# Another hand-written order of the same 2034 steps, with other engines for some splits and other buffers

## The chip, the cores and the metric

One NeuronCore of a Trainium2 chip runs the whole program. The metric is the device time of one execution in microseconds (us). Several executions are made; their median is the figure, and one further execution is recorded by the hardware profiler.

## The reference, cut to what matters

Two stages follow each other. In the first, for each of 8 batches and 8 heads, 512 tokens `x` of width 64 read 32 state rows by a softmax, and the 32 state rows read the tokens back. The two results, side by side, are 544 rows of width 512 for a batch. In the second stage four experts with a causal attention of width 64 work on these rows; a gate picks the two best experts for each row.

```python
scores = scale * x @ state.T;  xread = softmax(scores) @ state
sread = softmax(scale * state @ x.T) @ x
X = concat([xread, sread])                       # 8 x 544 x 512
logits = X @ w_gate; pick 2 of 4 experts, w = softmax of the two
for e in range(4):
    q, k, v = X @ wq[e], X @ wk[e], X @ wv[e]
    ye = softmax(causal(scale * q @ k.T)) @ v @ wo[e]
    out += w[:, e] * ye                          # only where e was picked
```

## The kernel before

The program is a list of 2034 steps, written batch by batch by ordinary Python functions: `first` and `front` (stage one of a batch and its q, k, v), `probs` (scores and exponentials of a block of 128 rows), `reads` (their product with v), `outs` (the product with wo and the store), `side` (the state rows) and `tail` (attention of the state rows of two batches). Each step has a number, an engine, one or a few instructions, and the buffers that it reads and writes. For some steps there are two or three ways to do it, on different engines: a number in float16 is kept as a high half (a rounded copy) and a low half (what is left of it), and `split`, `low`, `small` and `copy` let either ScalarE, VectorE or GpSimd make such parts.

What is issued when is not decided by these functions. `Steps.run` (lines 346 to 362) goes through the string `ORDER` and issues the steps in the order of its numbers. An entry `1929.0` is step 1929 by its way 0; `388.0.5` puts five matmuls of zeros ahead of step 388, which keep TensorE busy. All engines take their own instructions from this one list in its order, and each engine works through its part strictly in turn. The string table `SLOTS` says which of a tag's buffers each use takes: `"z": "1010..."` gives the first use buffer 1, the next one buffer 0, and so on. Semaphores are set by the tile framework from what reads and writes what.

```python
for entry in order:
    s = self.all[int(entry[0])]
    calls = s["ways"][int(entry[1])][2]
```

SyncE (SP) issues all DMAs, 172 of them, from one queue: loads of x, state and weights, stores of the output, and the transposing DMAs that bring high and low halves into the layout that TensorE needs (`xT<-xh`, `a2t<-a2`, `qm<-qh`, `pt<-ph`, `z<-zh`, `tpt<-ptl`). TensorE's products of the scores wait for `qm`, those with v for `pt`, those with wo for `z`.

Steps that the prediction names, with what they do: 62 and 63 load `wq` (three experts, then one), 64 and 65 `wk`, 66 and 67 `wv`, 68 the gate's weights. 86, 83 and 89 multiply `wk`, `wq` and `wv` with the state of batch 0; 119 is the first matmul after stage one's softmax of batch 0. 753 is a product with v in batch 2. 1440 to 1442 and 1455 to 1458 make the exponentials of two row blocks of batch 5, their high and low halves and the transposing DMA; 1479 is the product that reads the second of them. In the last batch 1926 to 1929 are high half, low half, transposing DMA and the product with wo of row block 3; 1969 and 1972 are the halves of the product with wo of row block 0; 1753 and 1756 are the products with wo of two blocks of batch 6. 2020 to 2022 are high half, low half and transposing DMA of the last tail's exponentials (`ptl`, `tpt`), 2023 is the product that reads them, 2031 the last product with wo, 2032 its copy and 2033 its store.

Of the kernel before, what the change touches and what calls it, by code (L numbers as in the profile page):

```python
# [125 lines left out]
    "p32": "02110221110211020210210210210210211021002",  # L126
    "mb": "00010101",
    "sbm": "10010010",
    "m2": "00001101",
    "bd": "0101010",  # L130
    "kt": "021012012",
    "gs1": "1001001010101",
# [1059 lines left out]
```

## Time and profile before

| | us |
|---|---|
| median of 3 executions | 288.12 (287.46 to 291.04) |
| profiled execution, its own time | 290.49 |
| its span, first to last instruction | 288.7 |
| granted TensorE clock, mean share of full speed | 0.994 |

The span is what the trace covers; 1.8 us of the execution's own time lie around it. A busy share of an engine is a mean over the whole span. The page of the profile gives busy times, a picture of the span in 40 slices, and the chain of waits that ended last. The other views ask the same trace for single stretches, engines and buffers.

### The profile page before, as it was taken

To read this page: it belongs to the slowest core of one execution; us is meant where nothing else is said; L and a number is where in the kernel's file an instruction comes from. 1 tells how busy PE (TensorE), PEld (TensorE's weight loads), DVE (VectorE), ACT (ScalarE), POOL (GpSimd) and SP (SyncE) were. 2 spreads that over 40 slices of the span, in tenths; PEclk is the share of its full clock that TensorE was granted. 3 is DMA by queue.
4 is the path that set the end of the run, shared out by engine and by line. 5 is a ranking of instruction groups with operands and counts; after the bars stand their busy time and mean duration, and the time that the engine had idled before them with its cause. 6 is when DMAs were issued, how large, how long until landed. Compare 5 with 4: busy or idle time off the path is not lost.

```text
span 288.7 us, 9583 instructions
## 1 busy us (share of the span) xinstructions
PE 270.6 (94%) x3571; PEld 182.2 (63%) x3573; DVE 242.5 (84%) x778; ACT 215.5 (75%) x707; POOL 197.9 (69%) x271
## 2 busy tenths in 40 slices
PE   8799998899899996999999999999999999999984
PEld 4757745486458643779457666776756667576742
DVE  2679999999899999899989899989899768887620
ACT  4488899798888889588889879657988475357632
POOL 7526986789768896489969969967687436616100
PEclk9979999999999999999999999999999999999999
DMA  7959779999999999989999999998559939899474
GB/s 194 180 166 128 171 198 159 246 165 185 259 173 206 199 184 165 246 222 201 227 179 233 155 254 244 204 226 165 142 129 130 220 85 146 165 181 156 123 210 148
DMA packets 154575, 53.20 MB, mean 184 GB/s; under 512 B 140576, under 2 KB 150048, under 8 KB 154528
## 3 DMA queue, kind: packets, MB, share of 16 engines
q1 hardware_dynamic: 154528, 52.59, 95.9%
q8 instruction: 28, 0.46, 0.6%
q14 instruction: 19, 0.16, 0.2%
HBM read 11.02 MB, written 8.91 MB: 69 GB/s over the span
## 4 chain that ended last, share of the span: by engine, by line
PE 60%; DVE 13%; DMA 12%; POOL 4%; ACT 4%; issue 3%; SPq 3%; DVEq 0%; ACTq 0%; POOLq 0%
PE bank L362 60%; DMA pt<-ph 6%; SPq L362 3%; DMA p<-in_moe_wk_dram 2%; DVE bank L362 2%; DMA qm<-qh 2%; DVE m L362 1%; DMA tpt<-ptl 1%; DVE z L362 1%; DVE qf L362 1%; DVE eb L362 1%; POOL z L362 1%; DVE xh L362 1%; DVE gs L362 1%; ACT p L362 1%
## 5 line engine op out<-in xcount | busy, mean ns | idle before, releaser
L362 PE MATMUL bank<-kt,qm 128*128 128x128 f16 (+13 forms) x368 | 48.2, 313 | 1.9 <-DMA qm<-qh 1.3
L362 PE MATMUL bank<-gs,at 128*128 128x260 f16 (+3 forms) x368 | 49.6, 282 | 0.4 <-ACT kt L362 0.2
L362 PE MATMUL bank<-v,pt 128*128 128x192 f16 x480 | 44.3, 246 | 5.3 <-DMA pt<-ph 4.3
L362 PE MATMUL bank<-wo_n,z 128*128 128x512 f16 (+1 forms) x198 | 46.2, 373 | 0.7 <-DVE gs L362 0.4
L362 PEld LDWEIGHTS <-pt 128*128 128x128 f16 x480 | 40.1, 97 | 9.2 <-DMA pt<-ph 6.5
L362 POOL TENSOR_TENSOR ph<-p,ph 128x256 f16<-128x256 f32 (+3 forms) x27 | 37.9, 1407 | 5.5 <-ACT bank L362 2.5
L362 PEld LDWEIGHTS <-at 128*128 128x128 f16 x336 | 32.4, 98 | 7.5 <-issue 1.1
L362 DVE CUSTOM_DVE_ANT_0 bank<-bank,causal 128x256 f32<-128x256 f32 (+3 forms) x64 | 30.2, 506 | 6.2 <-PE bank L362 5.4
L362 ACT ACTIVATE p<-bank,mx 128x384 f32<-128x384 f32 (+3 forms) x64 | 33.3, 524 | 1.3 <-DVE mx L362 0.2
L362 PEld LDWEIGHTS <-qm 128*128 128x128 f16 (+1 forms) x336 | 20.2, 96 | 17.9 <-issue 5.9
L362 PEld LDWEIGHTS <-z 128*128 128x128 f16 x198 | 18.6, 98 | 18.9 <-issue 1.4
L362 ACT ACTIVATE o<-bank 128x512 f32<-128x512 f32 (+1 forms) x35 | 20.2, 582 | 9.0 <-PE bank L362 7.3
L362 PE MATMUL bank<-at,gs 128*128 128x512 f16 (+1 forms) x100 | 24.4, 381 | 0.1
L362 DVE SCALAR_TENSOR_TENSOR xh<-xn,xh 128x512 f16<-128x512 f32 x23 | 18.5, 815 | 5.0 <-ACT xh L362 4.9
L362 POOL TENSOR_TENSOR z<-z 128x128 f32<-128x128 f32 x24 | 12.1, 504 | 14.9 <-DVE z L362 13.7
L362 DVE TENSOR_TENSOR z<-bank,c 128x384 f32<-128x384 f32 x32 | 17.5, 548 | 5.3 <-PE bank L362 3.1
L362 ACT ACTIVATE xh<-xn 128x512 f16<-128x512 f32 x32 | 19.5, 629 | 2.8 <-DMA xn<-in_x_dram 2.8
L362 POOL TENSOR_SCALAR ph<-p 128x768 f16<-128x768 f32 (+3 forms) x13 | 10.5, 804 | 15.2 <-ACT p L362 8.6
L362 POOL TENSOR_TENSOR qh<-qf,qh 128x384 f16<-128x384 f32 x18 | 17.3, 970 | 4.9 <-ACT qh L362 3.9
L362 POOL TENSOR_TENSOR zh<-z,zh 128x256 f16<-128x256 f32 x22 | 15.6, 714 | 6.8 <-DVE zh L362 3.3
L362 POOL TENSOR_TENSOR a<-e,a 128x512 f16<-128x512 f32 x14 | 16.5, 1184 | 4.1 <-ACT a L362 3.8
L362 DVE SCALAR_TENSOR_TENSOR qf<-bank,m 128x384 f32<-128x384 f32 x32 | 17.3, 549 | 2.1 <-PE bank L362 1.3
(206 smaller groups left out, 645.4 us busy)
## 6 DMA issues: line engine op xcount, KB each, us to landing
out_dram<-o SPq DMA_DIRECT2D x33, 256.0 KB, 3.1
xn<-in_x_dram SPq DMA_DIRECT2D x14, 512.0 KB, 4.5
xn<-in_x_dram SPq DMA_DIRECT2D x4, 256.0 KB, 4.0
sn<-in_state_dram SPq DMA_DIRECT2D x8, 64.0 KB, 3.7
p<-in_moe_wo_dram SPq DMA_DIRECT2D x2, 256.0 KB, 3.6
xT<-xh SPq DMA_TRANSPOSE x28, 4.1
pt<-ph SPq DMA_TRANSPOSE x25, 4.6
p<-in_moe_wk_dram SPq DMA_DIRECT2D x1, 384.0 KB, 5.5
```

The lines of the kernel that those rows point to most:

```text
L362: f(**{k: v.ap() if isinstance(v, View) else v for k, v in kw.items()})
```

## The change

Only the strings `ORDER` and `SLOTS` differ. Both orders hold the same 2034 steps once each. 117 of them go another way than before: 32 from VectorE to GpSimd and 11 back, 14 from ScalarE to GpSimd and 17 back, 26 from ScalarE to VectorE and 17 back. The fillers of zeros ahead of step 119 (three) are gone, and those ahead of step 388 are two and not five. On TensorE 232 of the 306 steps keep their order among each other, on SP 115 of 172. The diff, cut to the first lines, the last lines and some of the slots:

```diff
 ORDER = """
-2.0 3.0 184.0 186.0 32.0 52.0 0.0 47.0 51.0 7.0 34.0 61.0 33.0 39.0 38.0 40.0 13.0 48.0 71.0 1.0 8.0 69.0 4.0 5.0 131.0 9.0 187.0 72.1 185.0 10.0
-188.0 70.0 189.0 133.0 132.1 190.0 191.0 64.0 198.0 134.0 62.0 66.0 65.0 204.0 201.0 73.0 74.0 75.0 45.0 76.0 135.0 86.0 136.0 77.0 63.0 67.0 68.0
-207.0 83.0 218.0 6.0 88.0 87.0 78.1 137.0 195.0 138.0 89.0 210.0 79.0 91.0 80.1 44.0 50.0 324.0 139.0 222.0 140.0 141.0 142.1 323.0 322.0 90.0 325.0
...
-2013.0 1746.1 1911.0 1912.1 2014.0 1739.0 2015.0 2016.0 2017.0 2018.0 2019.0 2020.0 1740.0 1981.0 1942.1 1737.0 1909.0 1923.0 1922.0 1939.1 1940.0
-1924.0 1752.0 1945.0 1277.0 1941.0 1741.0 1954.0 1925.1 1926.2 1927.0 1753.0 1946.0 1947.1 1948.0 1756.0 1963.0 1943.0 1944.1 2021.1 1955.0 1956.0
-1949.0 1982.0 1950.0 1957.0 1951.0 1754.0 1958.0 1964.0 1965.0 1928.0 1966.0 1929.0 1967.0 1757.0 1968.0 2022.0 1755.0 1546.0 1959.0 1930.0 2023.0
-1952.0 1758.0 1738.0 1960.0 2024.0 2025.0 2026.0 2027.0 2028.0 2029.0 2030.0 1961.0 1969.0 1970.0 1953.0 1931.0 1962.0 1971.0 1972.0 1973.0 1974.0
-2031.0 2032.0 2033.0
+0.0 3.0 45.0 13.0 2.0 7.0 184.0 71.0 72.0 186.0 4.0 5.0 69.0 1.0 133.0 8.0 131.0 185.0 70.0 188.0 9.0 10.0 190.0 187.0 134.1 73.0 66.0 67.0 64.0 65.0
+62.0 132.0 135.0 204.0 207.0 198.0 189.0 191.0 74.0 75.0 63.0 6.0 68.0 136.0 323.0 322.0 86.0 201.0 76.0 83.0 20.0 32.0 48.0 14.0 33.0 15.0 77.0 11.0
+218.0 195.0 87.0 137.0 89.0 78.1 79.0 80.1 84.0 88.0 138.0 85.0 210.0 90.0 139.0 140.1 222.0 324.0 81.0 82.0 119.0 333.0 327.0 336.0 141.0 91.1 142.1
...
+1736.0 1934.0 1743.0 1977.0 2011.1 2012.0 1917.1 1919.0 1935.0 1544.0 1982.0 1749.1 1918.0 1920.0 1936.1 1937.0 1744.0 1745.1 2013.0 1938.0 1939.0
+1921.1 1750.0 1912.0 1746.0 1909.0 1923.0 1945.0 1940.1 2015.0 2014.0 1737.0 1922.0 1739.0 1954.0 1751.0 1752.0 2016.0 2017.1 1924.0 1925.0 1926.2
+1946.0 1942.1 1947.1 1941.0 1927.0 1948.0 1753.0 2018.0 2019.0 2020.0 1963.0 1545.0 1943.0 2021.1 1944.1 1955.0 1956.0 1964.0 1965.1 1949.0 1950.0
+1756.0 1957.0 1966.0 1951.0 1738.0 2022.0 1757.0 1754.0 1740.0 2023.0 1958.0 1952.0 1967.0 1968.0 1928.0 2024.1 1959.0 2025.0 2026.0 2027.0 1546.0
+1929.0 1972.0 1758.0 1741.0 1930.0 2028.0 2029.0 1973.0 1953.0 1755.0 2030.0 1960.0 2031.0 1961.0 1974.0 1931.0 1962.0 2032.0 2033.0 1969.0 1970.0
+1971.0
 """
 SLOTS = {
...
-    "a2t": "01010100",
-    "zh": "101110010110101",
-    "z": "101010010110100100",
+    "a2t": "10100110",
+    "zh": "010110111000101",
+    "z": "011101011001101100",
...
```

Of the steps that the prediction names, in words: the weights are loaded in the order 64, 62, 66, 65, 63, 67, 68 before and 66, 67, 64, 65, 62, 63, 68 after. TensorE's last steps before are 1756, 1963, 1957, 1951, 1966, 1929, 2023, 1960, 2028, 1969, 1972, 2031; after they are 1963, 1756, 1957, 1966, 1951, 2023, 1929, 1972, 2028, 1960, 2031, 1969. SP's end has 1741, 1928, 2022 before and 1738, 2022, 1928 after. On GpSimd 1456 now follows 1442 and stands ahead of 1457; before, ScalarE did it.

## Rows read from the trace of the kernel before

**Rows 1.** The page: busy us (share) xinstructions; TensorE's clock in 40 slices.
```profile
PE 270.6 (94%) x3571; PEld 182.2 (63%) x3573; DVE 242.5 (84%) x778; ACT 215.5 (75%) x707; POOL 197.9 (69%) x271
PEclk9979999999999999999999999999999999999999
```

**Rows 2.** Waits of PE: line <- releaser: us in total, times, longest.
```profile
PE bank L362 <- DMA pt<-ph: 4.3, 3, 2.9
PE bank L362 <- DMA p<-in_moe_wk_dram: 1.9, 1, 1.9
PE bank L362 <- DMA qm<-qh: 1.3, 1, 1.3
PE bank L362 <- DVE gs L362: 1.3, 2, 0.9
PE bank L362 <- DVE rd L362: 1.1, 2, 0.6
```

**Rows 3.** Windows: PE, PEld, DVE, ACT, POOL busy, clock, DMA, GB/s.
```profile
60.00:70.00 10.00, 9.94 (x179) 7.64 (x178) 9.93 (x27) 9.72 (x31) 8.60 (x11) 1.00 1.21 182
150.00:160.00 10.00, 10.00 (x142) 6.94 (x140) 9.50 (x33) 9.04 (x33) 10.00 (x9) 1.00 1.09 198
180.00:190.00 10.00, 10.00 (x104) 7.94 (x103) 8.77 (x38) 6.60 (x28) 9.55 (x13) 1.00 1.17 195
0.00:288.70 288.70, 270.59 (x3571) 182.21 (x3573) 242.47 (x778) 215.48 (x707) 197.93 (x271) 0.99 0.97 184
```

**Rows 4.** Timeline of PE, 12 to 21: start, us, instruction [idle].
```profile
14.86 1.53 PE L362 MATMUL bank<-p,tqf 64*32 64x256 f32 x32 [1.88 <-DMA p<-in_moe_wk_dram]
16.09 2.01 PE L362 MATMUL bank<-xT,tqf 64*32 64x512 f32 x16
19.60 0.81 PE L360 MATMUL bank<-zeros 128*128 128x512 bf16 x2
```

**Rows 5.** Windows of the head; the first of PE alone.
```profile
9.00:11.00 2.00, 2.00 (x22) 1.00 1.36 219
16.00:17.00 1.00, 1.00 (x20) 0.33 (x9) 0.98 (x2) 1.00 (x4) 0.44 (x2) 0.50 1.06 369
```

**Rows 6.** Timeline of PE: steps 1929, 2023, 1969 with 1972, 2031.
```profile
275.88 1.47 PE L362 MATMUL bank<-wo_n,z 128*128 128x512 f16 x6 [0.34 <-DMA z<-zh]
278.14 1.51 PE L362 MATMUL bank<-v,tpt 128*64 128x258 f16 x24 [0.80 <-DMA tpt<-ptl]
281.70 1.48 PE L362 MATMUL bank<-wo_n,z 128*128 128x256 f16 x12
283.02 1.46 PE L362 MATMUL bank<-wo_n,tz 128*128 128x512 f16 x6
```

**Rows 7.** Timeline of SP's queue, 265 to 289 us: steps 1928 and 2022.
```profile
273.38 1.19 SPq L362 DMA_TRANSPOSE z<-zh  x1
274.66 1.35 SPq L362 DMA_TRANSPOSE tpt<-ptl  x1
```

**Rows 8.** Waits of SP's queue, 265 to 289 us: total, times, longest.
```profile
SPq L362 <- PE bank L362: 3.9, 1, 3.9
```

**Rows 9.** Timeline of DVE, 266 to 274 us: step 2021.
```profile
270.43 0.79 DVE L362 TENSOR_TENSOR ptl<-p,ptl 128x640 f16<-128x640 f32 x1
```

**Rows 10.** Timeline of POOL, 212 to 220 us: steps 1441, 1442, 1457.
```profile
213.05 0.83 POOL L362 TENSOR_SCALAR ph<-p 128x768 f16<-128x768 f32 x1
213.97 1.65 POOL L362 TENSOR_TENSOR ph<-p,ph 128x768 f16<-128x768 f32 x1
216.61 2.13 POOL L362 TENSOR_TENSOR ph<-p,ph 128x1024 f16<-128x1024 f32 x1 [0.99 <-ACT ph L362]
```

**Rows 11.** Forms of two tiles: ns min/median/max, first and last start.
```profile
L362 POOL TENSOR_TENSOR zh<-z,zh x22: 667/672/1010, 57.9 to 269.4; 128x256 f16<-128x256 f32 x22
L362 DVE TENSOR_TENSOR zh<-z,zh x7: 383/424/641, 73.5 to 264.3; 128x256 f16<-128x256 f32 x7
L362 DVE SCALAR_TENSOR_TENSOR xh<-xn,xh x23: 647/691/2119, 5.8 to 185.0; 128x512 f16<-128x512 f32 x23
```

More of the change, by code (lines that the diff above doesn't have):

```diff
@@ L29 @@
 ORDER = """
[90 rows of a table removed]
[90 rows of a table added]
 """
 SLOTS = {
-    "xh": "3012031230210312",
-    "bank": ("014267350476321540517065102474703461701375402561732250376105237405612571430274653745063715067351237606105705731403576124"
-          "370165324076124764350132704216742065374602340512734051734063162713550273614250362514673104526365723153210345353261032617"
-          "03456216473025473047126530473623567035162735016045132740151476412753425734025734112034175372412536173425"),
[L126 to L129, printed above, removed]
-    "bd": "0101010",
-    "kt": "021012012",
-    "gs1": "1001001010101",
-    "s2": "10101010",
-    "lg": "0110010010101",
-    "gt1": "0101111111111",
-    "a2": "1010011010100101",
-    "gs2": "1000011011100",
-    "gw": "0100010010101",
-    "m6": "10101001",
-    "qf": "01010101101010010101101010101010",
-    "a2t": "01010100",
-    "qm": "11110000",
-    "wgt": "01010010",
-    "mx": "02001332033201320132013210321003",
-    "sums": "10101010",
-    "ph": "0102011210210211010211201",
-    "xt_tail": "1100",
-    "c6": "0000000101100110",
-    "z32": "01210121012012102101210102020210",
-    "zh": "101110010110101",
-    "z": "101010010110100100",
-    "qh": "10100101011001",
-    "o": "0120321210203221103021031302132102",
-    "tw2": "0110",
-    "m4": "0100",
-    "tmt": "1010",
-    "twg": "0100",
@@ new lines @@
+    "bank": ("045631753420671352240132075315231452163216704653120406231564031720565123510743120631402314032514725303405104520642135074"
+          "216705432167032542631607135620415670243650143715024371024362034106571453264107135267413607452036412506126154757160715162"
+          "47053120724650312756204563742063452106753261047520361702631673613405275310742530174720536145230124532067"),
+    "xh": "2301230123013201",
+    "p32": "01212002202120121020210210102100210120100",
+    "mb": "01011110",
@@ new lines @@
+    "sbm": "11100101",
+    "m2": "00010111",
+    "kt": "120102010",
+    "bd": "0101010",
+    "lg": "0001010101101",
+    "s2": "01010101",
+    "gs1": "0010010110010",
+    "gt1": "1011001010010",
+    "a2": "0101101010011010",
+    "gs2": "0110101010101",
+    "gw": "0101001010101",
+    "m6": "01010110",
+    "qf": "10101010101010011010100101011011",
+    "qm": "01010110",
+    "a2t": "10100110",
+    "wgt": "10010010",
+    "mx": "20132012301230123230231023012301",
+    "sums": "01001010",
@@ L158 @@
+    "ph": "1021201201201201201210210",
+    "c6": "0010110010101010",
+    "xt_tail": "0010",
+    "z32": "10201201012020101201201202102012",
+    "zh": "010110111000101",
+    "z": "011101011001101100",
+    "qh": "10010110101010",
+    "o": "0123211001232130321023031201320321",
+    "tw2": "0100",
+    "m4": "0010",
+    "tmt": "0010",
+    "twg": "0110",
     "tmx": "0101",
-    "tpt": "0111",
-    "tc4": "1010",
-    "tz": "01",
+    "tpt": "0101",
+    "tc4": "0101",
+    "tz": "00",
 }
```

163 rows, old and new, of the table ORDER are left out of this document.

## The prediction

> **What bounds the kernel.** The page comes first. PE is busy 94% of the span and no other engine over 84% [rows 1]. The clock is full but for the third slice, where the digit is 7, and the slices beside it. So the kernel is TensorE's, and what can be won is its idle time: 288.70 - 270.59 = 18.1 us [rows 3]. Some 4.2 of these lie behind the last matmul, which ends at 283.02 + 1.46 = 284.48 [rows 6], while its copy and its store run. The waits of PE name most of the rest: 4.3 us for `pt`, 1.9 for `wk`, 1.3 for `qm`, and 2.4 for small things of DVE [rows 2], 9.9 together, and 1.14 in the tail [rows 6]. All of them are transfers or parts that other engines bring too late, so an order can move them, and the matmuls themselves stay the same set. The windows show where the helpers set the pace: DVE is 99% busy from 60 to 70 us, POOL is full from 150 to 160 and 96% busy from 180 to 190, and in these last two PE loses nothing [rows 3].
>
> The sum below is made against the profiled execution, 290.49 us for a span of 288.7. That is 2.37 above the median of 288.12, so I take the difference over to the median and not the level.
>
> **The tail, worked out.** Step 1928, the transposing DMA of `z`, writes a buffer half that the product 1756 still reads. SP therefore sits 3.9 us in one wait for PE [rows 8] and issues 1928 at 273.38, and 2022 stands behind it and goes out at 274.66 [rows 7]. Its data were ready when 2021 ended, at 270.43 + 0.79 = 271.22 [rows 9]. PE starts on `tpt` at 278.14, 3.48 after the issue. The new order puts 2022 ahead of 1928, behind one store. It can then go out at about 271.3 and be there at 271.3 + 3.5 = 274.8. PE has the same work ahead of 1929 or 2023, whichever comes first, and is free at 275.88 - 0.34 = 275.54 [rows 6]: 0.7 us to spare, and the wait of 0.80 goes. 1928 still waits for 1756, which is now behind 1963, half a microsecond more. It goes out near 274.0 and lands 275.88 - 273.38 = 2.5 later, at 276.5; PE comes to 1929 after 2023, at 275.5 + 1.9 = 277.4, so the 0.34 goes as well. Late next would be 2028 and 2031, whose inputs come from 2023 over three small DVE steps; 1929 and 1972 stand between and cover them. Last, 1969 moves behind 2031. It is half of twelve matmuls of 1.48 [rows 6], so 2031 ends 0.74 earlier by that alone. Whether all of this counts depends on the store of 1969, which is now the last: with the same 4.2 us behind it nothing is won, with its half-size copy and store nearly all is. The tail gives between 1.14 and 1.88, and I take 1.8, since half the columns and half the bytes are nearest to the upper end.
>
> **The head.** [...] The whole of `wk` lay behind three loads of 384 KB and its own 128; now it lies behind `wv` and itself, 1.0 and not 1.3 MB. At the 219 GB/s of the row [rows 5] this is 1.2 us earlier, and 86 runs without a wait worth having. But 83 follows at once, and it needs all of `wq`, which was fifth of the six loads and is now sixth: 128 KB more at that rate, 0.6 us. PE's idle time moves from 86 to 83, while 86 leaves the stretch behind it. Before, the two took 1.53 together from 14.86 on [rows 4], and 83 was let go near 15.6. Now it is let go near 16.2, so what follows is 0.4 to 0.6 late, or earlier by up to 1.9 if the wait goes altogether. I take +0.4, by the row of the rate. The state, now behind x, costs nothing as long as the weights end the wait.
>
> The fillers ahead of 119 ran from 19.60 for 0.81 us, while PE would have waited [rows 4], so taking them away gives nothing. If the clock should fall for want of them, a stretch like that of the head at 0.50 [rows 5] would come again. A slice is 288.7 / 40 = 7.2 us, and its digit of 7 means 20 to 30% of the clock lost, 2.9 to 4.3 us at half speed [rows 1]; a second one would cost at most half of that, some 2. I take 0, as nothing else is idle there. The three fillers fewer ahead of 388 lie in a wait in the same way: 0.
>
> **The middle.** Ahead of the steps where PE waits longest the new order has the same matmuls but for one. 753, with the longest wait (2.9 for `pt`) [rows 2], has one product more and a short transposition less ahead of it, 0.66 - 0.11 = 0.55 of work, so its wait shrinks by 0.55. What brings `pt` there is not moved up: the same low half on POOL, and on SP again three plain issues between the last transposing DMA and it. Another wait can be followed by hand. 1456, ScalarE's before, now runs on POOL between 1442 and 1457. 1442 ended at 213.97 + 1.65 = 215.62; a high half of 1024 columns is 0.83 x 1024 / 768 = 1.11; 1457 would start at 216.73, and it started at 216.61 [rows 10]. That is the same, and 1479 waits as before.
>
> The engines' shares: DVE gives 32 steps to POOL and gets 11, and the low half of `zh` is the middle one of them, 0.42 on DVE and 0.67 on POOL [rows 11]. So DVE is relieved of some 21 x 0.42 = 9 us and POOL takes 7 to 14 (18 steps more at 0.4 to 21 at 0.67). Most of them belong to the batches from the fourth on, after 110 us, where PE hardly waits. From 30 to 70, where DVE sets the pace, its load stays within a microsecond. So the relief is worth nothing in the sum, between -5.1 (all that is left in [rows 2] without `wk` and the long wait: 1.4 + 1.3 + 1.3 + 1.1) and a loss, which is the third rival's. I take 0, because the loads move where nothing waits.
>
> [...] The subtraction `xh` takes 691 ns at the median and up to 2119 [rows 11]: something holds DVE up now and then. [...]
>
> **Sum.** -1.8 (tail) + 0.4 (head) - 0.55 (753) + 0 (fillers, loads) = -1.95, so 288.5 for a profiled execution like this one and 288.12 - 1.95 = 286.2 for the median.
>
> **Rivals.** First, the forecast: the ends change and the middle keeps its waits, 286.2, chance 0.46.
>
> Second, the middle gains too. The new order puts the parts of `pt` and `qm` ahead of work that can wait, and DVE's relief brings them in time. For it speaks that these waits are short, 0.9 to 1.3 each [rows 2]; against it, that DVE's and SP's queues ahead of the ones I followed hold the same work. All of 5.1 gives 286.2 - 5.1 = 281.1, and a head without its wait 1.9 + 0.4 less, 278.8. Chance 0.25.
>
> Third, slower: POOL becomes the late one from 150 us on. It is already full from 150 to 160 and at 9.55 of 10 from 180 to 190 [rows 3]. An addition of 7 to 14 us, where low halves for `pt` and `qm` come from POOL in order, makes a transposing DMA late by what POOL is behind. PE waits once this is more than the slack that it has there. It decides if two or more of the batches from the fourth to the seventh come some 4 us late: 2 x 4 = 8 less 1.95, 294. A single such wait gives 290. Chance 0.12 for the mechanism as a whole.
>
> Fourth, the change does nothing to the time: the tail's 1.8 is eaten by a fall of the clock without the fillers (+2), or by `wq` and a wait or two that are only somewhere else. 288, chance 0.17.
>
> **Numbers.** The likeliest is 286.2. Below 280.5 lies about a third of the second case, 0.08; above 290 most of the third, 0.1. The range is 280.5 to 290.0. Two per cent are 5.8 us, about what the runs of this kernel can tell from no change: 282.4 and 293.9 are the limits. Most of the second case and a little of the first lie below 282.4, 0.24; half of the third lies above 293.9, with some mishap of a kind that I don't see, 0.08; within, 0.68.
>
> **What would show it.** In the profile after: 2022 issued ahead of 1928 and no wait of PE for `tpt`; the last matmul a half-size one and some 4 us from it to the end; a wait for `wq` and not for `wk` near 14 to 16 us, with the clock at 0.50 behind it; about 2.3 us of wait for `pt` near 115, and 1.1 near 224. POOL's busy time should be 205 to 212 and DVE's near 233. The forecast is wrong if the waits for `pt` and `qm` are mostly gone (second), if PE waits from 150 us on for what POOL makes (third), or if the clock falls near 20 us (fourth).

## The result, and the profile after

The changed kernel takes 286.35 us (median of 20 executions, 284.58 to 287.47), the kernel before in the same rounds 288.89 (287.44 to 292.95). The ratio is 0.9905, interval 0.9878 to 0.9933: 2.7 us less (1.9 to 3.5), faster, by less than 2%. The forecast was 286.2.

The profiled execution of the changed kernel took 285.11 us, its span is 283.3. It lies 1.2 us under its median; the one of before lay 1.6 over the median of these rounds. The 5.4 us between the two spans are thus twice what the medians give, and no difference of these two traces alone is taken for the gain below.

The page after, the lines that answer to [rows 1] (busy us, share, instructions; the clock in 40 slices):

```profile
PE 267.1 (94%) x3567; PEld 181.2 (64%) x3567; DVE 233.2 (82%) x766; ACT 214.1 (76%) x692; POOL 210.3 (74%) x288
PEclk9999999999999999999999999999999999999999
```

DVE gave up 9.3 us and POOL took 12.4. The clock's 7 in the third slice is gone.

PE's waits after, which answer to [rows 2] (line <- releaser: us in total, times, longest):

```profile
PE bank L362 <- DMA pt<-ph: 3.1, 2, 2.2
PE bank L362 <- issue: 1.7, 1, 1.7
PE bank L362 <- ACT at L362: 1.7, 2, 0.9
...
PE bank L362 <- DVE rd L362: 0.9, 1, 0.9
PE bank L362 <- ACT p L362: 0.9, 1, 0.9
PE bank L362 <- DMA p<-in_moe_wq_dram: 0.8, 1, 0.8
```

`wk`, `qm` and `tpt` are gone, and of the three waits for `pt` one (1479); that at 753 went from 2.89 to 2.16, and that at 503 grew from 0.31 to 0.99. New are 1.7 us that the view calls issue (step 607, below), small waits for ScalarE, and 0.7 us for `z` at 512. From 150 us on the view lists no wait of PE at all.

The head, answering to [rows 4, 5]: PE's timeline, then windows (PE, PEld, DVE, ACT, POOL busy, clock, DMA share, GB/s):

```profile
14.62 0.67 PE L362 MATMUL bank<-p,tqf 64*32 64x256 f32 x16 [0.79 <-DMA p<-in_moe_wq_dram]
15.05 1.09 PE L362 MATMUL bank<-xT,tqf 64*32 64x512 f32 x16
18.15 1.13 PE L362 MATMUL bank<-at,gs 128*128 128x256 f32 x4 [0.79 <-ACT at L362]
```
```profile
15.00:17.00 2.00, 2.00 (x67) 1.39 (x48) 1.43 (x4) 2.00 (x9) 0.97 (x3) 1.00 1.08 367
```

The wait is for `wq` now, 0.79 and not 1.88, and the clock behind it is full in this execution.

The tail, answering to [rows 6, 7]: PE, then SP's queue:

```profile
271.77 1.51 PE L362 MATMUL bank<-v,tpt 128*64 128x258 f16 x24
273.11 0.50 PE L362 MATMUL bank<-tv,tpt 128*64 128x258 f16 x6
273.54 2.12 PE L362 MATMUL bank<-wo_n,z 128*128 128x512 f16 x12
275.60 0.45 PE L362 MATMUL bank<-both,tzr 128*64 128x64 f32 x8
275.98 1.47 PE L362 MATMUL bank<-wo_n,z 128*128 128x512 f16 x6
277.29 1.46 PE L362 MATMUL bank<-wo_n,tz 128*128 128x512 f16 x6
278.58 0.82 PE L362 MATMUL bank<-wo_n,z 128*128 128x256 f16 x6
```
```profile
266.25 1.33 SPq L362 DMA_TRANSPOSE tpt<-ptl  x1
270.18 1.19 SPq L362 DMA_TRANSPOSE z<-zh  x1
```

2022 goes out ahead of 1928, no line of PE has a wait, the half-size product is last and ends at 278.58 + 0.82 = 279.40, 3.9 us before the end. The last two stores, 2033 and then 1971 (the half-size one), each with its time from issue to landing:

```profile
279.40 0.60 SPq L362 DMA_DIRECT2D out_dram<-o  x1
DMA to landing us min/median/max: 2.5/2.5/2.5
280.10 0.54 SPq L362 DMA_DIRECT2D out_dram<-o  x1
DMA to landing us min/median/max: 2.1/2.1/2.1
```

2033 lands at 281.9 us, 1971 at 282.2, and the span ends 1.1 us behind that. In the kernel before, where 2033 is last, it ends 1.1 us behind 2033.

### The profile page after: what moved, and what is told of

Same layout as the page of the kernel before. It is cut to its first block, busy times and chain, and to the rows that moved or that the text cites. A ratio compares the mean times of both kernels' runs of the same rounds, so it can differ in the third digit from the quotient of the medians.

```text
span 283.3 us, 9569 instructions
## 1 busy us (share of the span) xinstructions
PE 267.1 (94%) x3567; PEld 181.2 (64%) x3567; DVE 233.2 (82%) x766; ACT 214.1 (76%) x692; POOL 210.3 (74%) x288
## 4 chain that ended last, share of the span: by engine, by line
PE 64%; DVE 13%; ACT 7%; DMA 6%; POOL 5%; issue 4%; SPq 0%; POOLq 0%; DVEq 0%; ACTq 0%
PE bank L362 64%; DMA pt<-ph 4%; DMA xn<-in_x_dram 2%; DVE bank L362 2%; ACT p L362 2%; DVE xh L362 2%; POOL ph L362 1%; DVE gs L362 1%; DVE qf L362 1%; DVE v L362 1%; DVE m L362 1%; DVE eb L362 1%; POOL eb L362 1%; POOL at L362 1%; ACT o L362 1%
## 5 line engine op out<-in xcount | busy, mean ns | idle before, releaser
L362 PE MATMUL bank<-gs,at 128*128 128x260 f16 (+3 forms) x368 | 50.3, 283 | 0.7 <-ACT e L362 0.4
L362 POOL TENSOR_TENSOR ph<-p,ph 128x256 f16<-128x256 f32 (+3 forms) x26 | 36.3, 1399 | 3.3 <-ACT ph L362 1.6
L362 DVE CUSTOM_DVE_ANT_0 bank<-bank,causal 128x128 f32<-128x128 f32 (+3 forms) x64 | 30.3, 505 | 7.5 <-PE bank L362 7.4
L362 ACT ACTIVATE p<-bank,mx 128x128 f32<-128x128 f32 (+3 forms) x64 | 33.3, 525 | 3.4 <-DVE mx L362 2.4
L362 PEld LDWEIGHTS <-z 128*128 128x128 f16 x198 | 18.7, 98 | 18.3 <-DMA z<-zh 1.3
L362 POOL TENSOR_TENSOR zh<-z,zh 128x256 f16<-128x256 f32 x28 | 19.5, 701 | 6.9 <-ACT zh L362 4.8
L362 DVE SCALAR_TENSOR_TENSOR xh<-xn,xh 128x512 f16<-128x512 f32 x24 | 16.9, 715 | 6.7 <-ACT xh L362 6.7
L362 POOL TENSOR_TENSOR z<-z 128x128 f32<-128x128 f32 x27 | 13.8, 515 | 8.9 <-DVE z L362 6.8
L362 POOL TENSOR_SCALAR ph<-p 128x1024 f16<-128x1024 f32 (+3 forms) x14 | 12.3, 876 | 9.4 <-ACT bank L362 4.5
```

What stands on the lines that cost most here:

```text
L362: f(**{k: v.ap() if isinstance(v, View) else v for k, v in kw.items()})
```

## The experiments

All were timed in five rounds against the kernel before, whose median on these chips was 290.7 to 292.6. "Order" and "engines" are the numbers and the ways in `ORDER`; buffers (`SLOTS`) go with the order except where that is said. Where a trace is compared, a step stands at the start of its first instruction, in us from the span's start as in the views. 453, 987 and 2013 have the same steps ahead of them on PE in both orders, so their starts cut the span into four comparable parts. The ratio of each run is the one on record, with its interval; it is not the quotient of the two medians.

**The last 104 steps.** e1 is the kernel before with its last 104 steps (from about 261 us) in the new order; e4 is the reverse.

```diff
 # e1: ORDER of before up to its position 1930, then
+... 2013.0 1938.0 1939.0 1921.1 ... 2022.0 1757.0 1754.0 1740.0 2023.0 ... 2033.0 1969.0 1970.0 1971.0
 # e4: ORDER of after up to its position 1930, then
+... 2013.0 1746.1 1911.0 1912.1 ... 1928.0 1966.0 1929.0 ... 2022.0 ... 2023.0 ... 2031.0 2032.0 2033.0
```

> The order of before with its last 104 steps (from about 261 us on) in the new order, by the new engines and buffers; all else as before. If the tail is what the change is worth, as forecast, PE no longer waits for tpt and z, the last product with wo ends 1.8 us earlier, and the ratio to before is 0.994 (1.8 of 289). If the gain was made ahead of the tail, from 110 to 235 us, this kernel stands at 0.998 to 1.000.

> The new kernel with its last 104 steps in the order of before, by the engines and buffers of before. If the tail is worth 1.8 us, it gives back 1.8: 0.997 to before. If the gain was made ahead of it, it stays at 0.990 to 0.993.

e1: 0.9983 (0.9942 to 1.0024). The interval holds both no gain and the 1.3 us that the trace shows from 2013 to the end of the span: 24.65 us against 25.97, without the two waits. e4: 1.0054 (1.0008 to 1.0100), some 4 us above the changed kernel and above both expectations. More than the tail came back: step 2013 itself waited:

```profile
265.08 2.77 PE L359 MATMUL bank<-kt,tq 128*64 128x512 f16 x12 [2.21 <-ACT p L359]
```

Its `tq` was ready at 261.60 us. What it waited for is its bank, which 1938, an exponential on ScalarE, freed at 264.94: at the joint 39 uses of buffers differ from the changed kernel. In this execution the clock also fell to 0.50 behind the wait, for 3.4 us. So e4 prices a bad joint along with the tail.

**The tail's three moves alone.** e5 takes them out of the changed kernel, e6 puts them into the kernel before.

```diff
 # e5, in after
-2022.0 1757.0 1754.0 1740.0 2023.0 1958.0 1952.0 1967.0 1968.0 1928.0 2024.1
+1757.0 1754.0 1740.0 1958.0 1952.0 1967.0 1968.0 1928.0 2022.0 1929.0 2023.0 2024.1
 # and 1969.0 directly ahead of 1972.0
 # e6, in before: 2022.0 ahead of 1928.0, 2023.0 ahead of 1929.0, and
-1969.0 1970.0 ... 2031.0 2032.0 2033.0
+2031.0 1969.0 1970.0 1971.0 2032.0 2033.0
```

> The changed kernel, with only its tail's three moves undone: the last transposition of tpt (2022) issued behind that of z (1928) again, its product (2023) behind 1929's, and 1969 ahead of 1972 and 2031. Theory: these three moves are what the tail gives, 1.3 us as e1's trace shows it from step 2013 to the end (26.2 to 24.9 us); undoing them costs about 1.3 us, ratio to the kernel before 0.995, and the trace shows a wait of 0.3 us for z and 0.8 us for tpt near the end again and a whole product last. Rival A: the tail's moves are worth nothing behind the new order, since something else ends last: 0.9905 as the changed kernel. Rival B: order, engines and buffers of the tail hang together, and any part undone costs as much as all of it (e4, 4 us): 1.005.

> The kernel before, with only the tail's three moves: 2022 issued directly ahead of 1928, 2023 ahead of 1929, and 1969 last on TensorE. Engines and buffers stay. Theory: 1.3 us less (1.1 to 1.9), ratio 0.995 (0.9935 to 0.9962); the trace has no wait of TensorE for tpt near the end, a half product last, and about 24.9 us from the start of 2013 to the end of the span against 26.2. Rival: the z transposition pushed behind 2022 becomes the late one, 1929 waits 1.2 us for it, and no more than the half product's 0.7 us is left: 0.9975.

e5: 1.0006 (0.9971 to 1.0040). Against the changed kernel's 0.9905 the moves are worth 2.9 us in the new order, more than twice what was expected. The trace names it; PE in the tail of e5:

```profile
275.61 1.47 PE L359 MATMUL bank<-wo_n,z 128*128 128x512 f16 x6 [0.87 <-DMA z<-zh]
277.85 1.51 PE L359 MATMUL bank<-v,tpt 128*64 128x258 f16 x24 [0.77 <-DMA tpt<-ptl]
281.00 1.47 PE L359 MATMUL bank<-wo_n,z 128*128 128x256 f16 x12 [1.31 <-DVE tz L359]
```

The waits for z and `tpt` are back, and there is a third: 1969 needs nothing of `tz`, so what it waits for is the bank that the new buffers give it, which DVE (step 1546) frees only there. 0.87 + 0.77 + 1.31 = 2.95; with the whole product last again, the part from 2013 to the end is 3.9 us longer than in the changed kernel (28.17 against 24.29).

e6: 0.9997 (0.9956 to 1.0039), which cannot tell 1.2 us from nothing. Its trace has none of the waits, but only 0.8 us less from 2013 to the end (25.20). The reason is my edit: 1970, the copy of the half product, came ahead of 2032 on ScalarE, and 2033, the full-size store, left behind the half-size one, at 282.87 us, and landed last, at 285.7. In the changed kernel 2033 stands ahead of 1970, and the two stores land 0.3 us apart, the half-size one last.

**Engines without order, order without engines.**

```diff
 # e2: ORDER of before, each number with the way it has in after, 117 of them, as
-1456.0
+1456.1
 # e10: ORDER of after, each number with the way it has in before
```

> The order, buffers and fillers of before, but the 117 steps go by the engines of the new kernel. If the engines count for nothing by themselves, as forecast, 1.000 within 0.003. If the relief of VectorE is what took the waits from 130 us on away, 0.993 to 0.996. If GpSimd becomes late where its work is not reordered as well, 1.005 to 1.02.

> The changed kernel's order with the engines of the kernel before for the 117 steps that changed theirs (the counterpart of e2, which had the new engines in the old order and was 6.8% slower). Theory: an order fits the engines that it was made with; steps that sit in another engine's queue hold it up, so this is slower too, by 3 to 8%: ratio 1.03 to 1.08. Rival: the order carries the gain and the engines are nearly free to choose: 0.99 to 1.00.

e2: 1.0684 (1.0629 to 1.0739), outside all that was expected. e10: 1.0337 (1.0276 to 1.0398), as its theory said. Either half alone costs more than the change brings. Both times PE waits longest for ScalarE's exponentials `p`, which is about half of the loss. PE's waits, e2, then e10:

```profile
PE bank L359 <- ACT p L359: 9.6, 10, 2.7
PE bank L359 <- DMA pt<-ph: 2.2, 2, 1.4
PE bank L359 <- POOL tq L359: 2.1, 1, 2.1
```
```profile
PE bank L359 <- ACT p L359: 4.8, 4, 1.8
PE bank L359 <- ACT o L359: 2.6, 2, 1.7
```

The changed kernel waits 0.9 us for `p`. How I read it: a step that goes to another engine stands in that engine's queue wherever the list has it, and what is behind it waits. No run moved single steps to show it.

**The head.** e3 is the kernel before with its first 150 steps in the new order and without the fillers at 119; e8b has only the loads of the weights in the new order; e7 is the changed kernel with the old fillers.

```diff
 # e8b, in before
-... 191.0 64.0 198.0 134.0 62.0 66.0 65.0 204.0 ... 63.0 67.0 68.0
+... 191.0 66.0 67.0 64.0 65.0 62.0 198.0 134.0 204.0 ... 63.0 68.0
 # e7, in after
-119.0 ... 388.0.2
+119.0.3 ... 388.0.5
```

> The first 150 steps (to about 25 us) in the new order with its engines, loads of weights and without the fillers ahead of step 119; the rest as before. The forecast said a head that is 0.4 us later: 1.001. If the head is 2.4 us earlier, as the one profile after shows at step 119, and this is kept, 0.992. If it is earlier and VectorE's full stretch from 30 to 70 us eats it, step 119 starts near 18 us and step 453 near 69.8 us as before, and the ratio is 0.998 to 1.000.

> The kernel before, with the loads of the weights in the new order: wv's two, wk's two, then wq's two, one behind the other ahead of step 198 (the last stays where 63 was). Nothing else. Theory: wk is there earlier, 1.9 us of wait at 16 us goes, the clock no longer falls behind it, and 119 starts up to 2 us earlier; but from 30 to 70 us VectorE is full and sets the pace, so that step 450 starts when it did: total unchanged, 1.000 (0.998 to 1.002). Rival A: the head's gain is carried to the end: 0.993. Rival B: wq, now last, is late instead, and 81 or 83 waits as long: no gain at 119 either.

> The changed kernel with the fillers of the kernel before added again: 3 products of zeros ahead of 119 and 5 in place of 2 ahead of 388. Theory: they fill time in which TensorE waits anyway or they are absorbed by the wait at the next full engine: no difference, 0.9905. Rival A: behind the new order of loads there is no wait left at 119, and the 3 fillers (about 0.9 us) lie on TensorE's path: 0.9935. Rival B: they keep the clock up in a stretch where the changed kernel's would at times fall: below 0.9905, by 1 us at most.

e3: 1.0263 (1.0207 to 1.0320), outside all that was expected and not usable for the question: 30 uses of banks differ from the kernel before, and one of them (step 293) made PE wait 2.0 us for DVE:

```profile
PE bank L359 <- DVE bd L359: 2.0, 1, 2.0
```

e8b is the clean one: 1.0022 (0.9992 to 1.0051), so loading each kind whole is worth nothing by itself. But it does not show the theory's reason. The wait for `wk` is gone, PE idles 0.95 us at 135 and 0.41 for `wq` at 83 in its place, and the clock falls behind that all the same (0.54 from 16 to 18 us), so 119 starts only 0.5 us earlier (20.00 against 20.54): rival B is nearer. And 453 starts 0.5 earlier too (69.55 against 70.08), so the little that was won was not eaten by then. e7: 0.9913 (0.9879 to 0.9946), the changed kernel's own ratio: the fillers cost nothing and save nothing.

**Where in the span.** e11 is the kernel before up to about 134 us, then the changed one.

```diff
 # ORDER of before up to its position 1022, then the rest as after has it
-1294.0 1133.0 1141.0 1554.0 1135.0 776.0 ...
+1294.0 786.0 1137.0 790.0 791.1 528.0 776.0 1133.0 ...
```

> The kernel before up to about 134 us, and behind that the steps in the order, on the engines and in the buffers of the changed kernel (two buffers of xh taken in another turn). Theory: the change's gain lies behind 134 us, in the waits at 1298, 1224, 987 and 1479, which all three old-order traces have (0.5, 0.8, 0.4 and 1.0 us) and no new-order trace has, and in the tail (1.2 us); the head and the stretch up to 134 us give nothing: ratio 0.9905 or a little under, 0.986 to 0.992, and the trace without those four waits. Rival A: the gain needs the whole order, and the joint at 134 us costs what the rest gives: 0.998 to 1.01. Rival B: only the tail counts: 0.9955.

e11: 0.9852 (0.9806 to 0.9897). All that the change brings, and perhaps a little more, is to be had behind about 134 us. Its trace has no wait at 1298, 1224 or 987; 0.6 us is left at 1479, and the joint cost 1.15 at 1133. Ahead of it are the old order's waits at 475 (1.57) and 753 (2.50), but 453 starts 1.3 us earlier than in the changed kernel. The starts and parts in us, with 1.70 (half of 3.4 us, an estimate) taken off the second part where the clock fell to 0.50 between 116 and 121 us (e1, e8b, e5, e7):

| kernel | start of 453 | 453 to 987 | 987 to 2013 | 2013 to end |
|---|---|---|---|---|
| before | 70.08 | 101.88 | 90.77 | 25.97 |
| e6, old order | 69.14 | 101.74 | 90.70 | 25.20 |
| e1, old order | 69.58 | 103.73 | 90.75 | 24.65 (new) |
| e8b, old order | 69.55 | 103.52 | 90.58 | 26.00 |
| after | 69.98 | 99.71 | 89.35 | 24.29 |
| e7, new order | 70.10 | 99.95 | 90.01 | 24.60 |
| e5, new order | 70.55 | 99.67 | 90.03 | 28.17 |
| e4, new order | 70.22 | 102.22 | (2013 waits) | 27.63 |
| e11, old then new | 68.64 | 102.90 | 89.93 | 24.32 |

The second part can be cut once more at 931, near 137 us, which also has the same steps ahead of it. Behind 931, up to 987, the four old-order traces take 36.0 us in the mean, after, e7 and e5 34.3, and e11 34.0; ahead of it, from 453 on, they take 66.7, 65.5 and 68.9. So the traces too have most of the gain where e11 has the new order.

**The longest wait.** In the changed kernel the data of 739, the transposition that 753 waits for, are ready when POOL ends 738, at 106.17 us, and it is issued at 109.09, behind three plain issues (the expectation of e9 has both times 0.23 lower, from another zero):

```profile
101.43 5.06 SPq L362 DMA_TRANSPOSE a2t<-a  x2
106.54 0.58 SPq L362 DMA_DIRECT2D xn<-in_x_dram  x1
107.17 0.66 SPq L362 DMA_DIRECT2D sn<-in_state_dram  x1
107.92 1.07 SPq L362 DMA_DIRECT2D out_dram<-o  x1
109.09 2.32 SPq L362 DMA_TRANSPOSE pt<-ph  x1
```

e9 and e12 reorder SP's queue there and nothing else (508 ahead of 1087 in both):

```diff
 # SP's part of ORDER
-... 706 1281 925 922 1282 1547 511 739     (after)
+... 706 1281 1282 925 922 739 1547 511     (e9)
+... 706 925 922 1281 1282 739 1547 511     (e12)
```

> The changed kernel with four transfers moved on SP's queue and nothing else: 739 (the transposition that 753 waits 2.2 us for) directly behind 922, ahead of 1547 and 511; 1282 ahead of 925; 508 ahead of 1087. Theory: in the changed kernel 739's data are ready at 105.93 us and it is issued at 108.86, three plain issues behind 922; issued at 106.9 it lands 2 us earlier, 753's wait falls from 2.2 to some 0.3 us, 512's 0.7 us goes, and the clock, which in other runs of this order falls to 0.5 for 3.4 us behind that wait (1.7 us lost), stays up: 2.5 to 4 us less than the changed kernel, ratio to the kernel before 0.977 to 0.982. Rival A: the transposition lands no earlier, since the DMA engines are full from 100 to 120 us: 0.9905 as the changed kernel. Rival B: the time comes back at the next wait (1298, 1197 or 1552's), as the head's did at 607 and 450: 0.987 to 0.9905.

> The changed kernel with SP's queue from 93 to 112 us mended: the transpositions 925 and 922, whose data are there at 86.3 and 98.8 us, ahead of the two loads of x (1281, 1282), these two together, 739 directly behind them, then 1547 and 511; 508 ahead of 1087. In e9 the loads of x went ahead, and the two transpositions behind them took 3.6 and 2.4 us to issue against 1.25 elsewhere, so that 926 waited 1.7 us in the place of 753. Theory: with the transpositions ahead, 926 waits no more, 739 issues at about 106 us, two to three us earlier than in the changed kernel, and 753 waits 0 to 0.6 us: 0.975 to 0.982 of the kernel before. Rival A: 739, now directly behind the loads, takes 3 to 4 us to issue and 753 waits 1 to 2 us again: 0.983 to 0.988. Rival B: PE's time won here is given back at a wait behind it (783, 1197, 1298), which e9's 0.5 us wait for z at 866 and 0.5 us at 783 point to: 0.982 to 0.985, as e9.

e9: 0.9828 (0.9775 to 0.9882). 753 waits no more, but 926 does, since the two transpositions behind the loads of x took 6.1 us to issue. For the same reason 739 left hardly earlier, at 108.89; but it landed 4.4 us behind its issue (113.25), where the changed kernel has 6.4 (115.44). What made it land sooner is not shown (PE, then SP):

```profile
111.39 1.08 PE L359 MATMUL bank<-xh,a2t 128*32 128x64 f16 x96 [1.72 <-DMA a2t<-a]
```
```profile
101.18 1.45 SPq L359 DMA_DIRECT2D xn<-in_x_dram  x2
102.67 6.12 SPq L359 DMA_TRANSPOSE a2t<-a  x2
108.89 2.26 SPq L359 DMA_TRANSPOSE pt<-ph  x1
```

e12: 0.9822 (0.9778 to 0.9866), median 286.54 against 290.69, a quotient of 0.986. The same views:

```profile
111.49 0.95 PE L359 MATMUL bank<-xh,a2t 128*32 128x64 f16 x96
...
115.01 0.66 PE L359 MATMUL bank<-v,pt 128*128 128x192 f16 x6
```
```profile
102.44 3.54 SPq L359 DMA_TRANSPOSE a2t<-a  x2
106.03 1.12 SPq L359 DMA_DIRECT2D xn<-in_x_dram  x2
107.45 3.51 SPq L359 DMA_TRANSPOSE pt<-ph  x1
```

Neither 926 nor 753 waits; from 453 to 753 PE takes 43.3 us (115.01 - 71.72) against 45.5 (115.48 - 69.98). Part comes back behind it, at 1298 (1.1), 780 (0.8) and 783 (0.7), so rival B is right in kind and the theory in the two waits; the ratio lies at the border of their ranges. e12 is the best version here by its ratio, with e9 and e11 inside its noise. It was not run beside the changed kernel: 0.9822 (up to 0.9866) and 0.9905 (from 0.9878) are both against the kernel before, in different rounds.

## Why the prediction was right

The number was right (286.2 for 286.35). Its terms were not all, and that they add up to it is in part luck.

**The tail, forecast -1.8.** Right, and a little smaller: from 2013 to the end 26.0 us in the kernel before and e8b, 24.3 to 24.7 in after, e7 and e1, so 1.3 to 1.7. Both waits went as worked out: 2022 left right behind 2021 and had time to spare, and 1928, pushed back, was still in time. The step's question, whether the store of 1969 decides, is answered: it does, but narrowly. Counted from 2013, 2033 lands 2.0 us earlier than before, and 1971 lands 0.35 behind it, which leaves 1.7. What I had not seen is how much the new buffers depend on these moves (e5: 2.9 us).

**The head, forecast +0.4.** The size in the end was near, the way was not. In the trace after, the wait for `wq` was 0.79 and the clock stayed up, so 119 started at 18.15 us, 2.4 earlier than before and not 0.4 later. Other executions of the new order differ: `wq` was waited for 0.59 (e7) to 2.21 us (e12), the clock fell behind it in e5 and e12 (0.50 from 16 to 18 us in both), and 119 came at 18.7 to 21.0. What the forecast had no term for is the stretch behind 119: from there to 453 after, e7 and e5 take 51.8, 50.9 and 50.7 us, the four old-order traces 49.5 to 50.4. 607 waited 1.73 us (0.15 before) for a transposition of x: its data came from POOL at 46.46 us, after POOL had idled 1.9 us for ScalarE (1.5 before), and the new order has another transposition ahead of it in SP's queue, so it left 0.86 later (0.03 before). And 450 waited 0.88 for DVE (0.59 before). At 453 the new order is 0.6 us behind (mean 70.21 of after, e7, e5 against 69.59). This is the new order's own loss, and not time that had nowhere to go: 607 waits 1.67 in e5 too, where 119 starts at 19.82; and in e11, with the old order there and no fall of the clock, 119 is 1.6 us earlier than before and 453 still 1.4.

**753, forecast -0.55, a wait of 2.3.** Right for the wait: 2.16, 2.32 and 2.33 us in after, e7 and e5. As a difference it is not shown: the traces with the old order there have 2.89, 2.06, 2.51, 3.60 and 2.50.

**The rest of the middle, forecast 0.** This is the term that failed. The step behind it is: "Ahead of the steps where PE waits longest the new order has the same matmuls but for one." I had checked that for 753 alone. Between 434, which makes the q that 475 multiplies, and 475, the new order has two more products (430 and 535, 0.8 us each), and the 1.2 us of wait that four old-order traces have at 475 (1.16 to 1.57) is zero in after, e5 and e7. At 1479 the chain on POOL went as forecast, 1457 right behind 1456 and that behind 1442:

```profile
210.04 1.65 POOL L362 TENSOR_TENSOR ph<-p,ph 128x768 f16<-128x768 f32 x1
211.65 1.04 POOL L362 TENSOR_SCALAR ph<-p 128x1024 f16<-128x1024 f32 x1
212.78 2.13 POOL L362 TENSOR_TENSOR ph<-p,ph 128x1024 f16<-128x1024 f32 x1
```

But 1675, 0.88 us of PE, now stands between the scores and the product that reads them, so PE comes 0.6 to 0.8 us later; the chain up to the issue is 0.3 shorter; and the transposing DMA landed 4.4 us behind its issue in after and e5, against 5.5 to 5.7 in the old order. The wait of 0.9 to 1.1 us fell to zero there, and to 0.5 in e7, where the DMA took 6.1. At 1298 one of the transpositions, 1294, moved from 134.9 us to 118.1, and 0.5 to 0.7 us of wait went. At 987 0.4 went, at 1224 part of 0 to 0.85. Against that stand the new order's own waits at 503 and 512. So the second rival was in part the truth: from 453 to 987 the four old-order traces take 102.7 us in the mean, after, e7 and e5 99.8 (with e4 100.4), and from 987 to 2013 90.7 against 89.8. That is 3.2 to 3.8 us, where I had 0.55. The scatter is large: e4, the same kernel in the second part, takes 102.2 there, more than e6 with 101.7. And not all of it is waiting: of the 2.9 us in the second part 1.8 are idle time of PE, and 1.1 are its busy time on the same matmuls (95.6 us against 96.8, fall of the clock taken off). What shortens that is not shown.

**The sum.** +0.6 - 3.5 - 1.5 is -4.4, and the medians say -2.7 (-1.9 to -3.5). Single profiled executions lie from 2.5 under (e3) to 2.8 over (e4) the median of their kernel, and the four old-order ones lie 1.0 over on average, after, e7, e5 0.2 under. That accounts for some 1.2 of the 1.7; the rest I can't settle from so few traces. e5 gives another estimate: its part from 2013 on is 2.2 us longer than in the kernel before, but its whole time is the same (1.0006, within 1.0 us), so the new order is worth 1.0 to 3.0 us ahead of 2013. There the forecast had 0.15 in all (+0.4 and -0.55). That it met the number is luck to this extent: a gain in the middle that it put at nothing, and traces that make the whole change larger than the medians do.

**The third and fourth rivals.** POOL's busy time is 210.3 and DVE's 233.2, inside the forecast; no wait of PE from 150 us on is listed, so none for POOL, and the third rival did not come about. Nor did the subtraction `xh` on DVE, whose longest time the forecast had noted, become slower. The trace after:

```profile
L362 DVE SCALAR_TENSOR_TENSOR xh<-xn,xh x24: 659/682/1168, 5.1 to 181.4; 128x512 f16<-128x512 f32 x24
```

682 ns at the median and 1168 at most, against 691 and 2119 [rows 11], with 12 us more on POOL. What made the longest one so long is not shown. The fourth needed a clock that falls without the fillers: e7 has them and takes the same time (0.9913 against 0.9905).

## What to carry to other kernels

A wait that goes is worth what the trace shows only if the new order makes no other behind it: here the 2.4 us that one trace won by 119 were gone at 453, at waits of the new order's own, and what was won behind 134 us stayed. To price a reordering, count for each wait the bound engine's work between the instruction that starts the chain and the one that reads its end, in both orders, and not only the chain. An order, its engines and its buffers are one thing (either half alone cost 3 and 7%), so take single moves out to learn what they are worth, and look at the DMA queue first: reordering four transfers of SP around one transposition brought some 0.5% (by the medians) to 0.8% (by the ratios) more, not measured side by side.

## What the runs showed of the hardware

**The clock fell in some executions and not in others, at the same places.** PE waited 2.89 us ahead of 753 before and 2.32 in e7. Windows behind it, before, then e7:

```profile
116.00:120.00 4.00, 4.00 (x44) 3.56 (x46) 3.31 (x7) 1.31 (x7) 1.50 (x2) 1.00 1.16 298
```
```profile
116.00:120.00 4.00, 4.00 (x27) 3.01 (x26) 3.04 (x8) 2.17 (x7) 2.95 (x4) 0.57 1.10 210
```

The shorter wait was followed by 3.4 us at 0.50, the longer by none. The same fall of 3.4 us came near 16 us, behind the wait for weights: in before, e1, e8b, e5 and e12, not in after, e6, e7, e9 or e11. The waits there were 1.36 us in all in e8b and 1.60 in e9, so again the longer one was not the one with the fall. Each costs up to 1.7 us (an estimate, half of 3.4), and a mean clock of 0.994 in place of 1.000 is one of them. Part of the scatter between executions of one kernel went with it: of 32 executions of the kernel before, timed in the rounds of e5 to e8b, the 8 with a mean clock of 0.996 or more took 290.8 us in the mean, the 7 under 0.992 293.3. What decides is not shown by these runs.

**Transposing DMAs behind loads took longer to issue in some places and not in others.** Half of the 102 in the changed kernel take 1.29 to 1.87 us on SP's queue; of the five directly behind a load of x four take 2.32 to 4.26. Directly behind the two loads of x, 512 KB each, the two transpositions `a2t` took 6.12 together (e9), ahead of them 3.54 (e12), and `pt`, then directly behind the loads, 3.51. But in the kernel before the first `a2t` behind one load of x took 1.26 and the second, behind the first, 3.73. The cause is not shown. Spreading the transpositions over a second engine's queue was not tried.
